# Two early row tiles instead of three in an attention kernel that hands its rows to a mixture of experts

## The chip, the cores and the metric

The kernel runs on one core of a Trainium2 chip. The metric is the device time of one execution in microseconds. Its engines are named TensorE (PE; its weight loads PEld), VectorE (DVE), ScalarE (ACT), GpSimd (POOL) and SyncE (SP). GpSimd and SyncE mostly issue transfers here.

## The reference

Attention over 8 batches, 12 heads, 448 tokens of 64 columns, with a root-mean-square norm of q and k, then a layer of 8 experts. Each token goes to the one expert that a hash of its id gives; the ids are inputs, so the table of rows is made on the chip.

```
q_n, k_n = rmsnorm(q, g_q), rmsnorm(k, g_k)
attn = softmax(scale * q_n @ k_n.T)
x = (attn @ v) as 3584 rows of 768 columns
expert_idx = token_ids * 2654435761 % 8
for e in range(8):
    mask = expert_idx == e
    h = relu(x[mask] @ w1[e])        # 768 -> 1024
    out[mask] = h @ w2[e]            # 1024 -> 768
```

## The kernel before

**Attention stage.** It walks 48 steps (8 batches of 6 pairs of heads). The order of all engines' work is written out by hand as a text of tokens (`steady`): `sc` scores, `exp`, `av` the output with the row sums, `rec` and `x` the normalisation into `x_sb`. TensorE, VectorE and ScalarE execute in that order; a transfer stands in the queue of the engine that issues it, and an engine that waits holds up what is queued behind it. After a batch's sixth step `put_x` calls `store_x`, which writes the batch's 448 rows to `x_scratch` in device memory. Partition p of the lower half holds the left columns of its seven tokens first, so the rows are stored as four pieces: three tokens from the lower 64 partitions, three from the upper, and the middle token's two halves. `put_x` ends with `hooks(s + 1)`, which issues loads and, near the end, gathers.

**Rows of an expert.** Every expert has 4 row tiles (KT) of 128 places (CAP = 512), of which 480 (FIT) are computed. The last tile is gathered as 96 rows. A table `gidx` holds the token of each place. Tokens of batches 0 to 6 come first, and those of batch 7 start at place EARLY or behind the earlier ones, whichever is later. So the tiles below EARLY hold no row of batch 7 and can be gathered before the last batch is stored. In a gather, N_EARLY as the row bound tells the framework that only rows of batches 0 to 6 are read; with N it waits for the last store. `gather` is an indirect DMA of GpSimd; `put_xT` turns a gathered tile with six transposes on TensorE and one copy (VectorE, or ScalarE where `nc.scalar.copy` is given).

**The seam.** The table of experts 0 and 1 is ready near the end of attention. Expert 0's early tiles are gathered by `hooks` into `xg_e` and turned by `early_xT`, ahead of the last step's `av`, in the PSUM banks of the scores. Then come the last `av`, `put_x` with the last store, and the gathers of expert 1's early tiles into `xg_ring`; then, in the expert stage, `fetch` of the tiles that need batch 7.

**Expert stage.** For each expert `gemm1` makes h, 8 blocks of 128 hidden units over the row columns; `gemm2` makes one row tile of the output in two parts (512 and 256 columns), evacuates it (ScalarE for even, VectorE for odd tiles) and scatters it. Expert 0 is special: `gemm1` covers the columns below EARLY, and `gemm1_late` the rest, right before its third row tile. `plan` says behind which block (`"g"`) or row tile (`"k"`) the work on the full table of experts 2 to 7 is emitted (p3 to p11, low, high, table_mm). `before` and `between` say what TensorE does before a row tile of `gemm2`, or between its two parts: mostly `turn`, the transposes of a row tile that is needed later (`t0` with the copy on ScalarE). All row tiles turned in this stage go through one PSUM bank (`ps_x`). Weights are loaded by GpSimd (`load_w1`, `load_w2`, `w_next`).

Of the kernel before, what the change touches and what calls it, by code (L numbers as in the profile page):

```python
# [13 lines left out]
AF = mybir.ActivationFunctionType  # L14
# [6 lines left out]
def kernel(  # L21
# [35 lines left out]
    EARLY = CAP - P  # L57
# [204 lines left out]
    with tc.manual_schedule(), \  # L262
# [369 lines left out]
        def early_xT(kt):  # L632
            bank = ps_sc.tile([P, 2, 512], FP32, name="sc_ps")[:, 0]
            put_xT(xg_e[:, kt], xT_e, kt, bank.bitcast(FP16)[:, 0:DIN],
                   nc.scalar.copy if kt == KT - 2 else None)
# [62 lines left out]
        def store_x(b):  # L698
# [3 lines left out]
            def rows(tok0, cnt, col, width):  # L702
                return bass.AP(tensor=x_dram.tensor, offset=(r0 + tok0) * DIN + col,
                               ap=[[SL * DIN, 64], [1, cnt * width]])
            nc.sync.dma_start(out=rows(0, 3, 0, DIN),
                              in_=x_sb[0:64, 0:6, :].rearrange("p a c -> p (a c)"))
            eng = nc.gpsimd if b == B - 1 else nc.sync
            eng.dma_start(out=rows(4, 3, 0, DIN),
                              in_=x_sb[64:P, 0:6, :].rearrange("p a c -> p (a c)"))
            nc.sync.dma_start(out=rows(3, 1, 0, HW), in_=x_sb[0:64, 6, :])  # L710
            eng.dma_start(out=rows(3, 1, HW, HW), in_=x_sb[64:P, 6, :])
# [80 lines left out]
        def hooks(s):  # L792
# [11 lines left out]
            if NS - 4 <= s < NS - 5 + KT:  # L804
                c = s - NS + 4
                gather(xg_e[:, c], gidx[:, c:c + 1], N_EARLY)
# [97 lines left out]
        for kt in range(KT - 1):  # L904
            early_xT(kt)
        for part in range(3):
            av_part(NS - 1, part)
        row_sums(NS - 1)
        put_x(NS - 1)
        for c in range(KT, 2 * KT - 1):  # L910
            gather(xg_ring[:, c], gidx[:, c:c + 1], N_EARLY)


    with tc.manual_schedule(), \
# [14 lines left out]
        def gemm1_late(w1v, xT, h_sb, c0, c1):  # L929
            n = c1 - c0  # L930
            for f0 in range(0, FO, 4):
                h_ps = ps_h.tile([P, 512], FP32, name="h_ps")
                for i in range(4):
                    for co in range(CO):
# [3 lines left out]
                nc.scalar.activation(h_sb[:, f0:f0 + 4, c0:c1],  # L938
                                     h_ps[:, 0:4 * n].rearrange("p (i t) -> p i t", i=4), AF.Relu)
# [43 lines left out]
        xgs = {c: xg_ring[:, c] for c in range(KT, 2 * KT - 1)}  # L983
        xTs = {0: xT_e}

        def fetch(e, kts):
            for kt in kts:
# [3 lines left out]
                                N_EARLY if kt < KT - 1 else N)  # L991
# [165 lines left out]
        def each(f, *parts):  # L1157
# [3 lines left out]
            (0, "g", 0): [tok16], (0, "g", 1): [p3], (0, "g", 2): [p4, p5], (0, "g", 3): [p6],  # L1161
            (0, "g", 4): [p7, p8], (0, "g", 5): [p9, p10, p11],
            (0, "g", 6): each(low, 0, 1), (0, "g", 7): each(low, 2, 3), (0, "k", 0): [high],
# [9 lines left out]
        before[0, 0], before[0, 1] = [t0(1, 0)], [t0(0, KT - 1)]  # L1173
        between[0, 1] = t0(1, 1)
# [4 lines left out]
        fetch(0, [KT - 1])  # L1179
        fetch(1, [KT - 1])  # L1180
# [78 lines left out]
```

## Time and profile before

| what | us |
|---|---|
| median of 3 runs (345.2 to 347.8) | 345.54 |
| profiled execution, its own time | 343.94 |
| its span, first to last instruction | 342.4 |
| TensorE busy in the span | 327.5 |
| VectorE, ScalarE, GpSimd busy | 201.8, 188.6, 147.7 |
| expert 0's first matmul starts | 163.26 |
| expert 1's first matmul starts | 186.50 |

The profile is one execution taken by the hardware profiler. Its span is 1.5 us shorter than the execution's own time. A busy TensorE says that matmuls were under way, not that they ran at their peak. Where an engine waits, the profile names what released it, or "issue" if it shows no wait. A landing time runs from the start of the issuing instruction to the completion of the transfer.

### The profile page before, as it was taken

How to read it: one execution, taken by the hardware profiler on the slowest of the kernel's cores; microseconds unless marked ns; L12 is line 12 of the kernel's file. 1: busy time of each engine (PE TensorE's matmuls, PEld its weight loads, DVE VectorE, ACT ScalarE, POOL GpSimd, SP SyncE). 2: the span in 40 equal slices, each digit the busy share in tenths (PEclk: the TensorE clock that was granted, in tenths of full speed). 3: DMA queues.
4: the chain of work that ended last, by engine and by line, in shares of the span. 5: the costliest groups of instructions: out<-in, count | busy, mean ns of one | idle time of the engine just before them, and what ended most of it. 6: DMA issues, size and time to landing. Idle time of an engine off the chain costs nothing. (4 is left out here: it accounts for less than half of the span.)

```text
span 342.4 us, 9198 instructions
## 1 busy us (share of the span) xinstructions
PE 327.5 (96%) x3893; PEld 228.6 (67%) x3893; DVE 201.8 (59%) x433; ACT 188.6 (55%) x286; POOL 147.7 (43%) x203
## 2 busy tenths in 40 slices
PE   4999999999999999999999999999999999999992
PEld 2577777776777777666677767677676776767761
DVE  3799999998989899976693243232332323323210
ACT  3599999999999999989442212212122120220210
POOL 8799935225330100003555854538555474202122
PEclk9999999999999999999999999999999999999997
DMA  8999999999999999032579899999999999403012
GB/s 138 217 200 202 202 236 200 239 202 227 201 244 211 254 210 233 13 82 71 127 147 247 169 204 249 261 278 244 252 272 262 259 243 278 174 0 133 22 79 88
DMA packets 42498, 64.80 MB, mean 189 GB/s; under 512 B 9687, under 2 KB 30623, under 8 KB 42200
## 3 DMA queue, kind: packets, MB, share of 16 engines
q0 software_dynamic: 38688, 58.09, 84.1%
q1 hardware_dynamic: 3456, 5.90, 5.6%
q8 instruction: 31, 0.51, 0.6%
q10 hardware_dynamic: 312, 0.21, 0.2%
q14 instruction: 11, 0.09, 0.1%
HBM read 89.29 MB, written 17.30 MB: 311 GB/s over the span
## 5 line engine op out<-in xcount | busy, mean ns | idle before, releaser
L642 ACT ACTIVATE expT<-sc_ps 128x896 bf16<-128x896 f32 x144 | 125.5, 973 | 1.6 <-PE sc_ps L626 1.3
L962 PEld LDWEIGHTS <-h_sb 128*128 128x128 f16 (+1 forms) x512 | 51.2, 104 | 30.0
L962 PE MATMUL o_ps<-w_sb,h_sb 128*128 128x512 f16 (+3 forms) x384 | 66.2, 326 | 0.0
L975 POOL DMA_INDIRECT out_dram<-o_sb,gidx x32 | 33.9, 1058 | 65.2 <-ACT o_sb L972 31.3
L949 ACT ACTIVATE h_sb<-h_ps 128x480 f16<-128x480 f32 (+1 forms) x36 | 19.9, 552 | 68.1 <-PE h_ps L945 68.1
L229 POOL DMA_INDIRECT kr<-x_scratch,gidx x32 | 33.5, 1047 | 52.1 <-DVE gidx L557 37.8
L945 PEld LDWEIGHTS <-w_sb 128*128 128x128 f16 x288 | 38.9, 136 | 16.2
L945 PE MATMUL h_ps<-xT,w_sb 128*128 128x480 f16 x240 | 49.4, 366 | 0.0
L972 ACT COPY o_sb<-o_ps 128x768 f32<-128x768 f32 x16 | 12.8, 798 | 61.4 <-PE o_ps L962 61.4
L951 DVE TENSOR_SCALAR h_sb<-h_ps 128x480 f16<-128x480 f32 x28 | 18.4, 658 | 47.2 <-PE h_ps L945 47.2
L626 PE MATMUL sc_ps<-qT,kT 64*128 64x448 f16 x288 | 44.5, 356 | 1.4 <-ACT expT L642 0.7
L660 PEld LDWEIGHTS <-expT 128*128 128x128 bf16 x864 | 37.8, 97 | 10.1 <-DVE x_sb L691 4.4
L660 PE MATMUL av_ps<-v,expT 128*128 128x65 bf16 x864 | 43.3, 193 | 0.1
L972 DVE COPY o_sb<-o_ps 128x768 f32<-128x768 f32 (+1 forms) x15 | 14.3, 956 | 31.5 <-PE o_ps L962 27.2
L691 DVE TENSOR_TENSOR x_sb<-av_ps,srec 128x448 f16<-128x448 f32 x48 | 29.9, 622 | 1.4
L303 POOL DMA_DIRECT2D vr<-in_v_dram x36 | 23.8, 671 | 15.6 <-DMA kr<-in_k_dram 6.8
L645 ACT ACTIVATE expT<-sc_ps 128x448 bf16<-128x448 f32 x48 | 29.4, 613 | 0.0
L384 PEld LDWEIGHTS <-ident 128*128 128x128 f16 x576 | 23.0, 99 | 8.5 <-issue 4.8
L241 DVE COPY xT<-xT_ps 128x768 f16<-128x768 f16 x25 | 13.8, 552 | 22.6 <-PE xT_ps L240 22.4
L665 PE MATMUL av_ps<-v,expT 128*128 128x130 bf16 x144 | 25.0, 220 | 0.0
L962 PE MATMUL o_ps<-kr,h_sb 128*128 128x512 f16 (+3 forms) x128 | 22.1, 326 | 0.0
L626 PEld LDWEIGHTS <-kT 64*128 64x128 f16 x288 | 12.6, 93 | 11.4 <-issue 2.5
(211 smaller groups left out, 453.0 us busy)
## 6 DMA issues: line engine op xcount, KB each, us to landing
w_sb<-in_moe_w_dram POOLq DMA_DIRECT2D x18, 512.0 KB, 10.9
w_sb<-in_moe_w_dram POOLq DMA_DIRECT2D x8, 768.0 KB, 13.7
kr<-in_k_dram POOLq DMA_DIRECT2D x7, 672.0 KB, 14.3
qr<-in_q_dram POOLq DMA_DIRECT2D x7, 672.0 KB, 12.5
x_scratch<-x_sb SPq DMA_DIRECT2D x15, 288.0 KB, 6.1
w_sb<-in_moe_w_dram POOLq DMA_DIRECT2D x2, 1536.0 KB, 26.5
qr<-in_moe_w_dram POOLq DMA_DIRECT2D x6, 512.0 KB, 15.6
vr<-in_v_dram POOLq DMA_DIRECT2D x14, 192.0 KB, 11.7
```

The source lines that it names most:

```text
L229: nc.gpsimd.indirect_dma_start(out=xg[0:idx.shape[0], :], out_offset=None, in_=x_dram[0:rows, :], in_offset=bass.IndirectOffsetOnAxis(ap=i ...
L303: eng.dma_start(out=dst[64 * half:64 * half + 64, :, s0:s0 + cnt, :].rearrange("p n s d -> p n (s d)"), in_=runs(t, h0 + HP * hh, 1, n, to ...
L626: nc.tensor.matmul(sc[:, hh, :S], lhsT=kT[64 * hh:64 * hh + 64, P * j:P * j + P], rhs=qT[64 * hh:64 * hh + 64, :], start=True, stop=True)
L642: nc.scalar.activation(expT[:, 2 * j:2 * j + 2, :], sc[:, :, :S], AF.Exp, bias=0.0, scale=1.0)
L645: nc.scalar.activation(expT[:, 6, :], sc[:, 0, :S], AF.Exp, bias=0.0, scale=1.0)
L660: nc.tensor.matmul(av[:, 2 * t + hh, :], lhsT=expT[:, tl(hh, j), P * t:P * t + P], rhs=v8[:, i, vs(hh, j), 0:D + 1], start=(hh == 0 and t ...
L665: nc.tensor.matmul(av[:, 2 * t:2 * t + 2, :], lhsT=expT[:, 6, P * t:P * t + P], rhs=v8[:, i, 0::7, 0:D + 1], start=False, stop=False)
L691: nc.vector.tensor_tensor(out=xs[b][:, :, hp * D:hp * D + D], in0=av[:, :, :D], in1=srec[:, :, None].to_broadcast([P, SL, D]), op=ALU.mult)
L945: nc.tensor.matmul(h_ps[:, :c1 - c0], lhsT=w1v[:, co, fo, :], rhs=xT[:, co, c0:c1], start=(co == 0), stop=(co == CO - 1))
L962: nc.tensor.matmul(o_ps[d0 > 0][0:w, d0:d1], lhsT=h_sb[:, fo, col * P:col * P + w], rhs=w2_sb[:, fo, d0:d1], start=(fo == 0), stop=(fo == ...
L972: (nc.vector.tensor_copy if col % 2 else nc.scalar.copy)(o_sb[0:w], o_ps[0][0:w])
L975: scat = nc.gpsimd.indirect_dma_start(out=out[:, :], out_offset=bass.IndirectOffsetOnAxis(ap=idx[0:w], axis=0), in_=o_sb[0:w], in_offset=N ...
```

## The change

EARLY falls from 384 to 256 places, so two tiles of each expert are free of batch 7 instead of three. Of expert 0 two tiles are gathered and turned ahead of the last step's output, and its third and fourth tile are gathered behind the last store; they are turned between the parts of `gemm2`'s first tile and before its second. `gemm1` of expert 0 covers 256 columns and `gemm1_late` 224, in four evacuations of two blocks. Expert 1's two early gathers are issued right behind the early transposes, ahead of the last step's output, and its other two tiles behind the last store. `store_x` writes three runs instead of four pieces, all from SyncE; in the last batch two of the four were GpSimd's. Pieces of the table's work move to other blocks of expert 0. For experts 2 to 7 the third tile's gather has the row bound N.

```diff
--- before.py
+++ after.py
@@ -54,7 +54,8 @@
     NOV = 32
     NHI = E * KT + NOV
     BIG = 1 << 20
-    EARLY = CAP - P
+    NE = KT // 2
+    EARLY = NE * P
     PL = P - P // B
     EH = E // 2
     KM = EH * NTC
@@ -632,7 +633,7 @@
         def early_xT(kt):
             bank = ps_sc.tile([P, 2, 512], FP32, name="sc_ps")[:, 0]
             put_xT(xg_e[:, kt], xT_e, kt, bank.bitcast(FP16)[:, 0:DIN],
-                   nc.scalar.copy if kt == KT - 2 else None)
+                   nc.scalar.copy if kt == NE - 1 else None)
 
         def expo(s, j):
             if j == 0:
@@ -702,13 +703,11 @@
             def rows(tok0, cnt, col, width):
                 return bass.AP(tensor=x_dram.tensor, offset=(r0 + tok0) * DIN + col,
                                ap=[[SL * DIN, 64], [1, cnt * width]])
-            nc.sync.dma_start(out=rows(0, 3, 0, DIN),
-                              in_=x_sb[0:64, 0:6, :].rearrange("p a c -> p (a c)"))
-            eng = nc.gpsimd if b == B - 1 else nc.sync
-            eng.dma_start(out=rows(4, 3, 0, DIN),
+            nc.sync.dma_start(out=rows(0, SL, 0, HW),
+                              in_=x_sb[0:64].rearrange("p a c -> p (a c)"))
+            nc.sync.dma_start(out=rows(4, 6, 0, HW),
                               in_=x_sb[64:P, 0:6, :].rearrange("p a c -> p (a c)"))
-            nc.sync.dma_start(out=rows(3, 1, 0, HW), in_=x_sb[0:64, 6, :])
-            eng.dma_start(out=rows(3, 1, HW, HW), in_=x_sb[64:P, 6, :])
+            nc.sync.dma_start(out=rows(3, 1, HW, HW), in_=x_sb[64:P, 6, :])
 
 
         def load(b, kinds="kqv"):
@@ -801,7 +800,7 @@
                 load(4, "kv")
             if hp == 3 and 1 <= b and b + 4 < B:
                 load(b + 4, "qkv")
-            if NS - 4 <= s < NS - 5 + KT:
+            if NS - 4 <= s < NS - 4 + NE:
                 c = s - NS + 4
                 gather(xg_e[:, c], gidx[:, c:c + 1], N_EARLY)
             if s == 24:
@@ -901,14 +900,14 @@
         """
         for b in range(2, B):
             emit(steady, b)
-        for kt in range(KT - 1):
+        for kt in range(NE):
             early_xT(kt)
+        for c in range(KT, KT + NE):
+            gather(xg_ring[:, c], gidx[:, c:c + 1], N_EARLY)
         for part in range(3):
             av_part(NS - 1, part)
         row_sums(NS - 1)
         put_x(NS - 1)
-        for c in range(KT, 2 * KT - 1):
-            gather(xg_ring[:, c], gidx[:, c:c + 1], N_EARLY)
 
 
     with tc.manual_schedule(), \
@@ -928,15 +927,16 @@
 
         def gemm1_late(w1v, xT, h_sb, c0, c1):
             n = c1 - c0
-            for f0 in range(0, FO, 4):
+            m = 512 // n
+            for f0 in range(0, FO, m):
                 h_ps = ps_h.tile([P, 512], FP32, name="h_ps")
-                for i in range(4):
+                for i in range(m):
                     for co in range(CO):
                         nc.tensor.matmul(h_ps[:, n * i:n * i + n], lhsT=w1v[:, co, f0 + i, :],
                                          rhs=xT[:, co, c0:c1],
                                          start=(co == 0), stop=(co == CO - 1))
-                nc.scalar.activation(h_sb[:, f0:f0 + 4, c0:c1],
-                                     h_ps[:, 0:4 * n].rearrange("p (i t) -> p i t", i=4), AF.Relu)
+                nc.scalar.activation(h_sb[:, f0:f0 + m, c0:c1],
+                                     h_ps[:, 0:m * n].rearrange("p (i t) -> p i t", i=m), AF.Relu)
 
         def gemm1(w1v, xT, h_sb, c0, c1, both=True, after=()):
             for fo in range(FO):
@@ -980,7 +980,7 @@
                 tc.declare_no_dep(scat.ins, group="scatters", reason="disjoint rows")
                 tc.add_to_no_dep_group("scatters", scat.ins)
 
-        xgs = {c: xg_ring[:, c] for c in range(KT, 2 * KT - 1)}
+        xgs = {c: xg_ring[:, c] for c in range(KT, KT + NE)}
         xTs = {0: xT_e}
 
         def fetch(e, kts):
@@ -988,7 +988,7 @@
                 c = e * KT + kt
                 xgs[c] = gather(xg_ring[:, c % (2 * KT)],
                                 gidx[0:P if kt < KT - 1 else LAST, c:c + 1],
-                                N_EARLY if kt < KT - 1 else N)
+                                N_EARLY if kt < NE else N)
 
         def turn(e, kt, copy=None):
             if e not in xTs:
@@ -1158,9 +1158,9 @@
             return [lambda p=p: f(p) for p in parts]
 
         plan = {
-            (0, "g", 0): [tok16], (0, "g", 1): [p3], (0, "g", 2): [p4, p5], (0, "g", 3): [p6],
-            (0, "g", 4): [p7, p8], (0, "g", 5): [p9, p10, p11],
-            (0, "g", 6): each(low, 0, 1), (0, "g", 7): each(low, 2, 3), (0, "k", 0): [high],
+            (0, "g", 0): [tok16], (0, "g", 1): [p3], (0, "g", 2): [p4, p5], (0, "g", 5): [p6],
+            (0, "g", 6): [p7, p8], (0, "g", 7): [p9, p10, p11] + each(low, 0, 1),
+            (0, "k", 0): each(low, 2, 3) + [high],
             (0, "k", 1): [high_tok], (0, "k", 2): [table_mm, lambda: fetch(2, range(KT))],
             (1, "k", 0): [overflow_table],
         }
@@ -1170,14 +1170,14 @@
         for e in range(1, E - 1):
             for kt in range(KT):
                 before[e, kt] = [t(e + 1, kt)]
-        before[0, 0], before[0, 1] = [t0(1, 0)], [t0(0, KT - 1)]
-        between[0, 1] = t0(1, 1)
+        before[0, 0], between[0, 0] = [t0(1, 0)], t0(0, 2)
+        before[0, 1], between[0, 1] = [t0(0, 3)], t0(1, 1)
         before[0, 2] = [lambda: gemm1_late(w1_view(0, w_tiles[0][0]), xTs.pop(0), hs[0], EARLY, FIT)]
         between[0, 2] = t0(1, 2)
         before[0, 3] = [t(1, 3)]
         hs = {}
-        fetch(0, [KT - 1])
-        fetch(1, [KT - 1])
+        fetch(0, range(NE, KT))
+        fetch(1, range(NE, KT))
         load_w2(2, w_tiles[2][1])
         queue += w_pieces(3)
         for e in range(E):
```

GpSimd's queue at the end of attention, with the semaphores each row waits for (kr_68 is `xg_e`, kr_69 is `xg_ring`; DMAHW are SyncE's stores, DMASW GpSimd's own transfers). Before:

```order
L229 DMA kr_68<-x_scratch,gidx 128x768 [waits DMASW3_49]
L708 DMA x_scratch<-x_sb 64x2304 [waits DMASW4_49,DVE_49]
L711 DMA x_scratch<-x_sb 64x384 [waits DMASW5_49]
L229 DMA kr_69<-x_scratch,gidx 128x768 [waits DMASW6_49]
L229 DMA kr_69<-x_scratch,gidx 128x768 [waits DMASW7_49]
L229 DMA kr_69<-x_scratch,gidx 128x768 [waits DMASW0_49]
L229 DMA kr_69<-x_scratch,gidx 96x768 [waits DMAHW3_49,DMASW5_49,DMAHW4_49,DMASW4_49,DMASW1_49]
L229 DMA kr_69<-x_scratch,gidx 96x768 [waits DMASW2_49]
```

The same place of the changed kernel:

```order
L230 DMA kr_68<-x_scratch,gidx 128x768 [waits DMASW2_49]
L230 DMA kr_69<-x_scratch,gidx 128x768 [waits DMASW3_49]
L230 DMA kr_69<-x_scratch,gidx 128x768 [waits DMASW4_49]
L230 DMA kr_69<-x_scratch,gidx 128x768 [waits DMAHW5_49,DMAHW6_49,DMAHW4_49,DMASW5_49]
L230 DMA kr_69<-x_scratch,gidx 96x768 [waits DMASW6_49]
L230 DMA kr_69<-x_scratch,gidx 128x768 [waits DMASW7_49]
L230 DMA kr_69<-x_scratch,gidx 96x768 [waits DMASW0_49]
```

The row that waits for the last batch's stores was the fourth behind them and is now the first behind two early gathers of expert 1; four tiles stand from it on instead of two.

TensorE between the two parts of `gemm2` of expert 0's first row tile, before:

```order
L962 LDWEIGHTS h_sb [waits Activation_49]
L962 MATMUL o_ps<-w_sb,h_sb 128x512
L962 LDWEIGHTS h_sb
L962 MATMUL o_ps<-w_sb,h_sb 128x256
L962 LDWEIGHTS h_sb
```

The same place of the changed kernel:

```order
L962 LDWEIGHTS h_sb [waits Activation_49]
L962 MATMUL o_ps<-w_sb,h_sb 128x512
L241 LDWEIGHTS kr_69 [waits DMASW5_49]
L241 MATMUL xT_ps<-ident_75,kr_69 128x128 [waits Activation_49]
L241 LDWEIGHTS kr_69
```

The transposes of expert 0's third tile stand between the parts now, and wait for the gather that waits for the stores.

## Rows read from the trace of the kernel before

**Rows 1.** Busy us (xcount) of PE, PEld, DVE, ACT, POOL; clock, DMA share, GB/s.
```profile
163.26:186.50 23.24, 23.15 (x231) 15.97 (x226) 16.33 (x39) 9.70 (x17) 13.38 (x12) 1.00 0.74 169
186.50:336.80 150.30, 149.04 (x930) 101.96 (x928) 45.50 (x70) 27.71 (x43) 68.54 (x76) 1.00 0.79 199
```

**Rows 2.** Timeline of TensorE at the seam: start us, length us, line, what, count.
```profile
161.35 1.00 PE L240 MATMUL sc_ps<-ident,kr 128*128 128x128 f16 x12 [0.41 <-DMA kr<-x_scratch,gidx]
...
162.19 0.53 PE L660 MATMUL av_ps<-v,expT 128*128 128x65 bf16 x12
...
163.26 2.12 PE L945 MATMUL h_ps<-xT_e,w_sb 128*128 128x384 f16 x12
...
165.22 0.22 PE L1051 MATMUL h_ps<-sel,onehot 128*112 128x2 bf16 x2
...
167.49 4.06 PE L945 MATMUL h_ps<-xT_e,w_sb 128*128 128x384 f16 x24
...
171.65 0.51 PE L240 MATMUL xT_ps<-ident,kr 128*128 128x128 f16 x6
...
171.99 2.77 PE L962 MATMUL o_ps<-w_sb,h_sb 128*128 128x512 f16 x16
...
174.59 0.50 PE L240 MATMUL xT_ps<-ident,kr 128*128 128x128 f16 x6
...
177.87 2.20 PE L935 MATMUL h_ps<-xT_e,w_sb 128*128 128x96 f16 x48
...
179.91 1.89 PE L962 MATMUL o_ps<-w_sb,h_sb 128*128 128x512 f16 x8
...
186.50 9.88 PE L945 MATMUL h_ps<-xT,w_sb 128*128 128x480 f16 x48
```

**Rows 3.** Timeline of TensorE's weight loads, third early tile.
```profile
161.84 0.34 PEld L240 LDWEIGHTS <-kr 128*128 128x128 f16 x6 [0.15 <-DMA kr<-x_scratch,gidx]
```

**Rows 4.** Timeline of ScalarE: last exp, copy of the third early tile.
```profile
161.03 0.62 ACT L645 ACTIVATE expT<-sc_ps 128x448 bf16<-128x448 f32 x1
...
162.39 0.80 ACT L241 COPY xT_e<-sc_ps 128x768 f16<-128x768 f16 x1 [0.74 <-PE sc_ps L240]
```

**Rows 5.** Timeline of VectorE: index table, last x, end of the routing's work.
```profile
154.29 0.33 DVE L557 CAST gidx<-val 64x8 int32<-64x8 f32 x2
...
163.61 0.62 DVE L691 TENSOR_TENSOR x_sb<-av_ps,srec 128x448 f16<-128x448 f32 x1
...
183.76 0.21 DVE L1138 TENSOR_SCALAR emp<-h_ps 128x56 f32<-128x56 f32 x1 [3.04 <-PE h_ps L1136]
```

**Rows 6.** Timeline of SyncE's queue: its two pieces of the last store.
```profile
164.26 0.45 SPq L705 DMA_DIRECT2D x_scratch<-x_sb  x1
...
164.75 0.60 SPq L710 DMA_DIRECT2D x_scratch<-x_sb  x1
```

**Rows 7.** Timeline of GpSimd: the first two gathers.
```profile
154.92 1.13 POOL L229 DMA_INDIRECT kr<-x_scratch,gidx  x1 [37.75 <-DVE gidx L557]
...
156.35 1.02 POOL L229 DMA_INDIRECT kr<-x_scratch,gidx  x1 [0.30 <-issue]
```

**Rows 8.** The gathers' line L229, 154 to 173 us (eight gathers); POOLq is GpSimd's sequencer.
```profile
L229 POOLq EVENT_SEMAPHORE  x2: 43/996/1948, 167.4 to 169.4; - x2
...
DMA to landing us min/median/max: 2.9/3.8/5.0
```

**Rows 9.** The same view, first gather alone, then the second alone.
```profile
DMA to landing us min/median/max: 3.2/3.2/3.2
...
DMA to landing us min/median/max: 5.0/5.0/5.0
```

**Rows 10.** Tile x_sb, its stores: SyncE's last two; the last four; all 32.
```profile
DMA to landing us min/median/max: 2.9/3.0/3.1
...
DMA to landing us min/median/max: 2.9/3.3/3.8
...
DMA to landing us min/median/max: 2.9/6.2/8.6
```

## Prediction

> **What bounds the kernel now.** I read the busy time by stretches first, since a share of the whole says nothing of one seam [rows 1]. From the first matmul of expert 0 to that of expert 1 TensorE works 23.15 of 23.24 us, and from there to its end 149.04 of 150.30 us, all at granted clock 1.00. TensorE is the bound on both sides of the edit, so only TensorE's own work or waits there change the end; what the other engines save is worth nothing.
>
> Then TensorE's order of time at the seam [rows 2]. The reader is to see two gaps and the pace of each kind of work. The gaps: transposes of early tile 1 begin only at 161.35 us, released by their gather, and the first transposes of expert 1 at 171.65 us, although the 24 matmuls from 167.49 us are out by 167.49 + 24 x 0.1633 = 171.41 us; 0.24 us are lost there. The pace: 12 matmuls of 384 columns take 163.26 to 165.22, 0.1633 us each; 48 of 96 columns 177.87 to 179.91, 0.0425 each; six transposes 171.65 to 171.99, 0.34; a pass of gemm2 171.99 to 174.59, 2.60, two thirds of it (1.73) the 512 columns and 0.87 the 256.
>
> Last I read the chain that the change leans on, attention output to gathered rows: VectorE ends the last x at 163.61 + 0.62 = 164.23 [rows 5], SyncE stores at 164.26 and 164.75 [rows 6], GpSimd's gathers follow [rows 7, 8], and the landings [rows 8 to 10].
>
> **Part 1, one early tile less ahead of the last step.** Six transposes leave the place before the last attention output. Tile 1 still waits to 161.35 [rows 2], as its gather keeps its place and its 5.0 us [rows 7, 9]. Before, tile 2's weight loads began at 161.84 [rows 3] and the output's matmuls 0.35 later, at 162.19 [rows 2]; now they follow tile 1 by the same 0.35, at 161.70. Gain 0.49 us, and gemm1 starts at 163.26 - 0.49 = 162.77. ScalarE bounds the gain: its last exp ends at 161.65, the copy of the last early tile takes 0.80 and ended 0.07 ahead of gemm1 [rows 4], so gemm1 can't start before 162.52, a gain of 0.74 at most; if tile 1's gather lands 0.5 later, since two gathers stand behind it instead of one, it is 0. I take 0.49, as the landing of the same gather is in the trace. The six transposes come back between the halves of gemm2's first pass: +0.34.
>
> **Part 2, other columns.** Expert 0's columns split 256 + 224 instead of 384 + 96. At the pace of the 384-column row, 48 x 0.1089 = 5.23 and 48 x 0.0953 = 4.57, together 9.80; before 48 x 0.1633 + 2.04 = 9.88. That is -0.08; by the 96-column pace for the late ones (0.0425/96 x 224 = 0.0992 each) it would be +0.11. The four evacuations of the late part instead of two are ScalarE's, each under 12 matmuls (1.14 us) against some 0.6 us: nothing while that cover stands.
>
> **Part 3, expert 1's gathers ahead.** They leave GpSimd right behind the two early ones [rows 7], near 157.8 us, and with even 5.0 us [rows 9] land five microseconds ahead of need, so the 0.24 us go. VectorE's table work keeps its order, and it stood idle 3.04 us for TensorE at its end [rows 5]: that cover hides the regrouped plan.
>
> Without any new wait the sum is -0.49 + 0.34 - 0.08 - 0.24 = -0.47 us.
>
> **Part 4, the new wait.** Expert 0's tiles 2 and 3 are now both gathered behind the store of the last batch, and needed sooner. TensorE comes to tile 2 at 162.77 + 5.23 + 0.31 (the routing's small matmuls: 171.65 - 163.26 - 48 x 0.1633 - 0.24) + 0.34 + 1.73 = 170.38 us. The rows come: x ends at 163.74; SyncE issues at 163.77, 164.26 and 164.90 (0.49 and 0.60 + 0.04 apart [rows 6]). A store on this queue, idle at this place, took 2.9 to 3.1, with GpSimd's two 2.9 to 3.8 [rows 10]; the last piece is the small one, whose row is the 2.9: it lands at 167.8. GpSimd stands waiting there, where before its sequencer's wait of 1.95 us to 169.4 lay under the gathers ahead [rows 8]. From the index table's end at 154.62 [rows 5] to its gather at 154.92 [rows 7] a release took 0.30, so the first late gather starts at 168.1. The first gather of a burst on an idle queue landed after 3.2 [rows 9]: 171.3, and TensorE waits 0.9. The second starts 1.43 later [rows 7], at 169.5; the two nearest prices are 5.0 (second of that burst [rows 9]) and 2.9 (the shortest of eight), and I take the median of the eight, 3.8 [rows 8]: 173.3. TensorE is there at 171.3 + 0.34 + 0.87 = 172.5 and waits 0.8. Together 1.7 us.
>
> Bounds of this term: with store 2.9, no release time and 2.9 for each gather, the second lands at 167.8 + 1.43 + 2.9 = 172.13, against 171.59 of an unstalled TensorE: 0.54. With 3.8 for the last store and 5.0 for the second gather it lands at 168.7 + 0.3 + 1.43 + 5.0 = 175.4: 3.8. The start of gemm1 shifts both sides alike and doesn't change it. Behind the waiting gather on GpSimd stand three gathers, expert 2's w2 load and the scatters; expert 1's late tiles are needed some 8 us after they land, w2 two experts later, and the scatters are waited for by nobody here, so nobody else waits.
>
> All batches' stores now have three pieces instead of four. None of them is waited for in the attention stage, where SyncE has nothing else to issue; if that cover were gone, 7 x 0.6 us of issue saved would be the most it could give. I take nothing.
>
> **Sum:** -0.47 + 1.7 = +1.2 us. The profiled execution's own time is 343.94 us, 1.5 around its span of 342.4 and 1.6 below the median of 345.54; I put the difference on the median: 346.8 us. About 1% (3.5 us) is what a measurement of this kernel can tell from no change.
>
> **Rivals.** (a) The late rows land in time. TensorE would have to find tile 2 by 170.38 and tile 3 by 171.59; the shortest prices (170.7 and 172.13) miss by 0.3 and 0.5. For it: the store's packets are longer and nothing else is under way. Against it: not one of eight gathers was below 2.9. It gives -0.47, 345.1 us. The Trainium skill, "DMA: Bandwidth & Descriptors", section "Anatomy of one DMA — SWDGE (gpsimd) path", puts a DMA at some 2.0 us plus its bytes at 436 GB/s. Estimated by that rule the 48 KB store would take 2.1 and a gather of 192 KB 2.45, the rows would land at 169.8 and 171.2, and this rival would hold; the trace disagrees, with 2.9 for that store and 3.2 for the quiet gather. Chance 0.20.
>
> (b) Slower: the two dependent DMAs at their long ends. The mechanism is the same chain, store, release, second gather, at 3.8 and 5.0, and with the gain of part 1 gone as well: +0.02 + 3.8 = +3.8, 349.3 us. It decides for slower from tile 3 landing 3.9 us after the unstalled TensorE comes for it (with part 1's gain kept). For it: the second gather of the one quiet burst did take 5.0, and stores in the loaded attention stage took 6.2 in the median and up to 8.6 [rows 10]. Against it: no load is under way here. Chance 0.10.
>
> (c) The change doesn't shorten the front: tile 1's landing slips to where tile 2's was, and all else goes as forecast. +0.49 more, 347.3 us. Chance 0.10.
>
> **How the numbers follow.** The forecast (wait of 0.5 to 3 us, 345.5 to 348) has 0.57; something unseen that gains over 1% has 0.03, as no row shows 3.5 us to be had. 8 times in 10: from rival (a) and a little of run scatter, 344.9, to near the upper bound, 348.9. Within 1% lie the forecast, (a) and (c): 0.87; slower 0.10, faster 0.03.
>
> **What the new profile would show.** gemm1's 256-column matmuls from about 162.8; no idle ahead of expert 1's first transposes; SyncE's three stores from 163.8; a GpSimd gather released by a store near 168; TensorE idle some 0.9 and 0.8 us before the transposes of expert 0's tiles 2 and 3; expert 1's first matmul near 187.7 instead of 186.50, and the rest of the program equal. I am wrong if no idle stands before those transposes (a), if it exceeds 3.9 us (b), or if the later experts' stretch changes its 150.30 us.

## The result, and the profile after

| | median us | ratio to before, 95% interval |
|---|---|---|
| kernel before | 345.72 | |
| changed kernel | 349.26 | 1.0101 [1.0073, 1.0128] |
| changed kernel, timed a second time (before 344.52) | 347.07 | 1.0075 [1.0053, 1.0097] |

The change makes the kernel slower: 3.5 us in the first comparison, 2.6 us in the second. The forecast was +1.2, and 348.9 us as the upper end; 349.26 lies above it. What both intervals allow is 1.0073 to 1.0097, +2.5 to +3.3 us.

Where it is lost shows first in the busy time by stretches of the changed kernel (columns as in [rows 1]): expert 0's first matmul to expert 1's first, then from there on to the end of the later experts' work.

```profile
167.69:193.06 25.37, 23.64 (x236) 18.83 (x232) 15.86 (x39) 10.84 (x20) 11.35 (x9) 1.00 0.65 146
193.06:343.20 150.14, 149.05 (x930) 101.93 (x928) 45.52 (x70) 27.71 (x43) 68.44 (x76) 1.00 0.79 200
```

The second stretch is as long as before (150.30 in [rows 1]). In the first TensorE, idle for 0.09 of 23.24 us before, is idle for 1.73 of 25.37. Its timeline there answers to [rows 2]:

```profile
167.69 1.49 PE L945 MATMUL h_ps<-xT_e,w_sb 128*128 128x256 f16 x12
...
173.60 1.89 PE L962 MATMUL o_ps<-w_sb,h_sb 128*128 128x512 f16 x8
177.21 0.51 PE L241 MATMUL xT_ps<-ident,kr 128*128 128x128 f16 x6 [1.72 <-DMA kr<-x_scratch,gidx]
177.56 1.04 PE L962 MATMUL o_ps<-w_sb,h_sb 128*128 128x256 f16 x8
178.60 0.49 PE L241 MATMUL xT_ps<-ident,kr 128*128 128x128 f16 x6
178.94 1.89 PE L962 MATMUL o_ps<-w_sb,h_sb 128*128 128x512 f16 x8
...
181.87 4.76 PE L935 MATMUL h_ps<-xT_e,w_sb 128*128 128x224 f16 x48
...
193.06 1.18 PE L945 MATMUL h_ps<-xT,w_sb 128*128 128x480 f16 x5
```

The wait stands where the forecast put it, ahead of the transposes of expert 0's third tile: the eight 512-column matmuls are out by 173.60 + 1.73 = 175.33, the transposes begin at 177.21, 1.88 later (the row's 1.72 counts from the modelled end of the last matmul). Ahead of the fourth tile's transposes nothing waits for a gather. The 0.17 us lost there (177.56 + 0.87 = 178.43 to 178.60) go to the one PSUM bank that both tiles are turned through: ScalarE's copy of the third tile empties it at 177.75 + 0.80 = 178.55 (ScalarE's timeline):

```profile
177.75 0.80 ACT L242 COPY xT_e<-xT_ps 128x768 f16<-128x768 f16 x1 [3.16 <-PE xT_ps L241]
```

The cause of the wait for the third tile is in the queues. SyncE's timeline (answers to [rows 6]):

```profile
168.69 0.45 SPq L706 DMA_DIRECT2D x_scratch<-x_sb  x1
169.18 0.60 SPq L708 DMA_DIRECT2D x_scratch<-x_sb  x1
169.82 1.01 SPq L710 DMA_DIRECT2D x_scratch<-x_sb  x1
```

GpSimd's timeline, the first early gather and the first two late ones (answers to [rows 7]):

```profile
156.37 1.13 POOL L230 DMA_INDIRECT kr<-x_scratch,gidx  x1 [37.76 <-DVE gidx L558]
...
174.10 1.00 POOL L230 DMA_INDIRECT kr<-x_scratch,gidx  x1 [12.65 <-DMA x_scratch<-x_sb]
175.40 0.98 POOL L230 DMA_INDIRECT kr<-x_scratch,gidx  x1 [0.30 <-issue]
```

From the first store's issue to the gather that the stores release are 5.41 us. The forecast had 4.33 (163.77 to 168.1).

One thing in this execution is not part of the change. In the last attention steps VectorE stands still for 2.46 us, ScalarE for 1.66 and TensorE for 2.00, and TensorE's granted clock is 0.50 behind it (163.20 to 166.62), 1.2 of 2.4 GHz. TensorE's timeline:

```profile
163.19 0.84 PE L661 MATMUL av_ps<-v,expT 128*128 128x65 bf16 x12 [2.00 <-DVE x_sb L692]
```

Call the time from the start of the first gather to expert 0's first matmul the front, and that from there to expert 1's first matmul the seam. No other profile of a changed kernel has the standstill; all have a front of 7.74 to 7.78 us, against 163.26 - 154.92 = 8.34 before and 11.32 here. The parts of the change are therefore read from the second execution of the unchanged file, below.

### The profile page after: what moved, and what is told of

Same layout as the page of the kernel before. It is cut to its first block, busy times and chain, and to the rows that moved or that the text cites. A ratio compares the mean times of both kernels' runs of the same rounds, so it can differ in the third digit from the quotient of the medians.

```text
span 348.8 us, 9194 instructions
## 1 busy us (share of the span) xinstructions
PE 329.6 (95%) x3893; PEld 232.8 (67%) x3893; DVE 201.9 (58%) x432; ACT 190.2 (55%) x289; POOL 147.5 (42%) x201
## 5 line engine op out<-in xcount | busy, mean ns | idle before, releaser
L949 ACT ACTIVATE h_sb<-h_ps 128x480 f16<-128x480 f32 (+1 forms) x36 | 19.0, 528 | 66.3 <-PE h_ps L945 60.3
L945 PE MATMUL h_ps<-xT,qr 128*128 128x480 f16 x96 | 19.8, 366 | 0.0
```

What stands on the lines that cost most here:

```text
L945: nc.tensor.matmul(h_ps[:, :c1 - c0], lhsT=w1v[:, co, fo, :], rhs=xT[:, co, c0:c1], start=(co == 0), stop=(co == CO - 1))
```

## Experiments

Two families: names with b_ are the kernel before with one part of the change, names with a_ are the changed kernel with one thing undone or doubled. Medians of before differ by up to 1.2 us from one set of runs to another, so ratios are compared.

### Parts of the change alone: b_store3 and b_burst4

b_store3 gives the kernel before the three-run store and nothing else; b_burst4 only sends expert 1's first gather out ahead of the last output.

```diff
# b_store3, against before: store_x as in the change
-            eng = nc.gpsimd if b == B - 1 else nc.sync
...
+            nc.sync.dma_start(out=rows(3, 1, HW, HW), in_=x_sb[64:P, 6, :])
# b_burst4, against before
             early_xT(kt)
+        gather(xg_ring[:, KT], gidx[:, KT:KT + 1], N_EARLY)
...
-        for c in range(KT, 2 * KT - 1):
+        for c in range(KT + 1, 2 * KT - 1):
```

> The kernel before with the three runs of the store from SyncE alone, nothing else. GpSimd has no store between its gathers any more, so six gathers stand in a row: three of expert 0 and three of expert 1. Burst theory: the front, 8.3 us before from the first gather to gemm1, grows by as much as in the changed kernel or more (to 11 us or above), and the time is 2 to 4 us above before. Rival (the stores, or nothing): the front stays within 0.7 us of 8.3, and the time within 0.7 us of before; if the shorter stores cost the attention stage something, its earlier batches are later too.

> The kernel before with expert 1's first gather issued ahead of the last step's output: four gathers in a row, the store with GpSimd as before, three early tiles. Burst theory: the front grows from 8.3 by 1 to 3 us, the time is 1 to 3 us above before although the 0.24 us wait ahead of expert 1's first transposes is gone. Rival: the front stays, and the time is 0 to 0.5 us below before.

Measured: b_store3 0.9992 [0.997, 1.0013], b_burst4 0.9995 [0.9974, 1.0016], both with the front at 8.18 us and the seam at 22.97. Neither part by itself costs anything that can be measured, and a burst of six gathers ahead of the output doesn't lengthen the front, so the burst theory falls here. Both seams are 0.27 us shorter than before, near the 0.24 of part 3. The chain is as long in b_store3 as in the changed kernel: SyncE's first issue at 163.96, the released gather at 169.30, 5.34 us. Only nobody waits for it there, since the kernel before needs those rows later (timeline of GpSimd, b_store3):

```profile
169.30 1.09 POOL L229 DMA_INDIRECT kr<-x_scratch,gidx  x1 [6.83 <-DMA x_scratch<-x_sb]
```

The four pieces on two queues are no sooner where they are kept: in b_burst4 x ends at 164.51 and the released gather starts 5.68 us later (GpSimd's timeline, b_burst4); in the profiles of the changed kernel it is 5.44 and 5.65.

```profile
170.19 0.98 POOL L229 DMA_INDIRECT kr<-x_scratch,gidx  x1 [1.53 <-DMA x_scratch<-x_sb]
```

### Fewer early gathers: a_burst3

```diff
-        for c in range(KT, KT + NE):
-            gather(xg_ring[:, c], gidx[:, c:c + 1], N_EARLY)
+        gather(xg_ring[:, KT], gidx[:, KT:KT + 1], N_EARLY)
```

> The changed kernel with three gathers in a row ahead of the last step's output, as before, instead of four: expert 1's second tile is gathered behind the store. Burst theory (four gathers back to back hold up TensorE, VectorE and ScalarE in the last steps of attention): the time from the first gather's start to gemm1's first matmul, 8.3 us before and 11.3 in the changed kernel, falls back to 8.3 or less, and the time falls by 1 to 2 us below 349.3. Rival (that loss is not of the burst: it belongs to the run, to the code's place, or to the stores): it stays near 11 us where it was, or comes and goes with no regard to the count of gathers, and the time stays within 0.7 us of 349.3.

Measured: 1.0080 [1.0048, 1.0111], no better than the changed kernel. The profiled execution is the slowest of six (350.17 us, median 347.68), and in it the wait is not shorter but longer. Timeline of TensorE, a_burst3:

```profile
174.79 0.51 PE L241 MATMUL xT_ps<-ident,kr 128*128 128x128 f16 x6 [2.85 <-DMA kr<-x_scratch,gidx]
...
176.73 0.82 PE L241 MATMUL xT_ps<-ident,kr 128*128 128x128 f16 x6 [0.56 <-DMA kr<-x_scratch,gidx]
177.35 3.05 PE L961 MATMUL o_ps<-w_sb,h_sb 128*128 128x512 f16 x8
```

Busy time of a_burst3 by stretches, the granted clock third from the end:

```profile
171.80:174.80 3.00, 0.15 (x2) 0.02 (x2) 2.97 (x4) 0.00 (x0) 2.69 (x2) 1.00 0.22 66
174.80:177.00 2.20, 1.64 (x17) 1.29 (x18) 2.20 (x3) 1.59 (x2) 1.78 (x2) 0.84 0.21 57
177.00:180.00 3.00, 3.00 (x13) 1.33 (x11) 0.69 (x1) 0.81 (x2) 2.50 (x3) 0.55 0.45 124
180.00:182.00 2.00, 2.00 (x22) 1.77 (x21) 0.35 (x1) 0.80 (x1) 1.52 (x2) 1.00 1.05 158
```

So the burst theory falls: the front is 7.74 us again, and with one gather fewer ahead of it the last store landed 3.8 us after its issue, at 170.03, as it does in the changed kernel (3.7, below). What was longer in this execution is the way from that landing to the gather, 1.6 us instead of 0.8; why stays open. Timeline of GpSimd, a_burst3:

```profile
171.63 1.00 POOL L230 DMA_INDIRECT kr<-x_scratch,gidx  x1 [11.46 <-issue]
```

A second cost appears, which no term of the forecast holds: behind the wait the granted clock falls to half, 1.2 of 2.4 GHz, and the eight 512-column matmuls take 2.89 us instead of 1.73, the transposes 0.62 instead of 0.34: 1.44 us more. It is not in every execution: this one has a mean granted clock of 0.993 and one other 0.989 (349.08 us), the remaining four 0.996 to 0.997 and 346.4 to 347.9 us.

### The late rows needed later: a_turn_later

```diff
-        before[0, 0], between[0, 0] = [t0(1, 0)], t0(0, 2)
-        before[0, 1], between[0, 1] = [t0(0, 3)], t0(1, 1)
+        before[0, 0], between[0, 0] = [t0(1, 0)], t0(1, 1)
+        before[0, 1], between[0, 1] = [t0(0, 2)], t0(0, 3)
```

> The changed kernel with one thing moved: TensorE turns expert 0's tiles 2 and 3 one place later each (expert 1's second tile takes the place between the halves of the first pass). Chain theory (the rows that wait for the store are late by 1.9 us, and that is the seam's loss): TensorE comes 1.2 us later to tile 2, so the wait falls from 1.7 to about 0.5 us or less; expert 0's stretch, first matmul to expert 1's first matmul, falls from 25.4 to near 24 us, and the time is 1.0 to 1.9 us below the changed kernel's 349.3, near 347.8. Rival (the loss of the changed kernel lies ahead of expert 0, between the gathers' issue and gemm1): the time stays within 0.7 us of 349.3, and the trace shows again some 3 us more than before from the first gather to gemm1.

Measured: 1.0017 [0.9999, 1.0036]. Two lines of order, with every store and gather left as it is, take back most of the loss, as the chain theory expected. A wait of 0.82 is left, and the seam is 188.93 - 164.45 = 24.48 us (TensorE's timeline):

```profile
174.28 0.51 PE L241 MATMUL xT_ps<-ident,kr 128*128 128x128 f16 x6 [0.82 <-DMA kr<-x_scratch,gidx]
```

### The changed kernel again, and with TensorE kept busy: a_again, a_fill

```diff
# a_again: the changed kernel, nothing edited
# a_fill: ahead of the third tile's transposes
+            for _ in range(10):
+                nc.tensor.matmul(ps[:], lhsT=ident16[:], rhs=hs[0][:, 0:2, 0:EARLY],
+                                 start=True, stop=True)
```

> The changed kernel itself, for a second trace. In its first trace the engines stood still for some 3 us ahead of expert 0 (from the first gather to gemm1 11.3 us), in the two variants with the same front they did not (7.7 us). Chain theory: the front is 7.7 us again, 0.6 below before, and expert 0's stretch is 26 to 28.5 us against 23.24 before: TensorE waits 2 to 3 us for the first gather behind the store, and its granted clock is at half for some microseconds after the wait. Rival (the front loses 3 us in most runs): the front is above 10 us again, and expert 0's stretch near 25.4.

> The changed kernel with ten matmuls of 512 columns, 2.16 us, that nobody reads, in front of the transposes that wait for the first late tile. They keep TensorE at work through most of the wait. Theory A (the wait costs twice: its own time and the clock that is at half behind it, 1.2 to 1.5 us): the clock stays at 1.00 through expert 0's stretch, and the time is 0.5 to 1.5 us below the changed kernel of the same call. Theory B (only the wait itself costs): the time is the same, or up to 0.5 us above where the wait is shorter than 2.16 us.

Measured: a_again 1.0075 [1.0053, 1.0097], a_fill 1.0058 [1.0035, 1.008]. TensorE's timeline in a_again, where the front has no standstill:

```profile
170.08 1.89 PE L962 MATMUL o_ps<-w_sb,h_sb 128*128 128x512 f16 x8
173.95 0.51 PE L241 MATMUL xT_ps<-ident,kr 128*128 128x128 f16 x6 [1.98 <-DMA kr<-x_scratch,gidx]
```

The same place in a_fill:

```profile
171.69 2.32 PE L1176 MATMUL h_ps<-h_sb,ident 128*128 128x512 f16 x10
173.85 0.50 PE L241 MATMUL xT_ps<-ident,kr 128*128 128x128 f16 x6
```

Both seams are 25.6 us (25.63 and 25.64): matmuls that nobody reads fill the wait and move nothing. The front is 7.74 us again, as expected for a_again, but the fallen clock that was expected with it isn't there: the clock is 1.00 all through this seam, so here the wait alone is the seam's loss. With TensorE kept busy the loss is 346.75 - 344.52 = 2.2 us, 0.3 less than without, which the intervals can't tell from nothing.

The three stores are the transfer that the wait is made of. DMA share and GB/s are the last two numbers of these stretches of a_again; the first store was issued at 165.18:

```profile
165.00:166.00 1.00, 1.00 (x15) 0.92 (x13) 0.28 (x2) 0.85 (x3) 0.00 (x0) 1.00 0.00 0
166.00:167.00 1.00, 1.00 (x12) 0.90 (x10) 0.90 (x6) 0.46 (x2) 0.00 (x0) 1.00 0.81 172
167.00:168.00 1.00, 1.00 (x11) 0.90 (x10) 0.86 (x6) 0.59 (x2) 0.00 (x0) 1.00 0.93 172
168.00:169.00 1.00, 1.00 (x13) 0.90 (x12) 0.79 (x7) 0.56 (x2) 0.00 (x0) 1.00 0.96 311
169.00:170.00 1.00, 1.00 (x14) 0.92 (x12) 0.93 (x3) 0.43 (x2) 0.00 (x0) 1.00 0.17 49
```

172 + 172 + 311 + 49 is 704 thousand bytes in some 3.2 us with the 16 DMA engines busy: nearly all of it the last batch's x (336 + 288 + 48 KB, 688 thousand bytes). The small third store, 48 KB, stands behind 624 KB. It was issued at 166.31 and landed 3.7 later, at 170.02; the two ahead of it landed 3.4 and 3.9 after their issue, the second at 169.53. The gather they release starts at 170.80. The stretch cut where the bytes start and stop to move:

```profile
166.20:169.45 3.25, 3.25 (x34) 2.92 (x32) 2.77 (x18) 1.69 (x5) 0.00 (x0) 1.00 0.89 217
```

So of the 5.62 us from the first issue to the released gather 1.02 pass before bytes move, 3.25 move them at 217 GB/s, 0.57 go by to the last landing (170.02) and 0.78 from there to the gather.

### VectorE or the issuing engine as the cause: a_table_late, a_act_store

The first moves VectorE's routing work behind the wait, in case it delays GpSimd's release; the second lets ScalarE issue the small third store.

```diff
# a_table_late
-            (0, "g", 6): [p7, p8], (0, "g", 7): [p9, p10, p11] + each(low, 0, 1),
-            (0, "k", 0): each(low, 2, 3) + [high],
+            (0, "k", 0): [p6, p7, p8, p9, p10, p11] + each(low, 0, 1, 2, 3),
# a_act_store
-            nc.sync.dma_start(out=rows(3, 1, HW, HW), in_=x_sb[64:P, 6, :])
+            (nc.scalar if b == B - 1 else nc.sync).dma_start(out=rows(3, 1, HW, HW), in_=x_sb[64:P, 6, :])
```

> The changed kernel with VectorE's work on the full table (from the rank on) moved behind the first pass of gemm2, so that VectorE is idle while GpSimd waits for the store and gathers the late tiles. Theory A (VectorE's work delays GpSimd: the gather starts 0.8 to 1.5 us after the store's landing where 0.3 was expected, and gathers take 1.7 to 2.3 us on GpSimd where 1.0 is usual): start after 0.3 to 0.5, each gather 1.0, TensorE's wait 0.5 to 1.2 us shorter, and the time 0.5 to 2 us below the changed kernel. Theory B (the delay is GpSimd's own): starts and lengths stay, the time stays within 0.5 us or is up to 1 us longer, if the table comes too late for its matmuls.

> The changed kernel with the last batch's third and smallest run of the store issued by ScalarE beside SyncE's two. Theory A (the store's landing is late because three issues stand in one queue, the third 1.13 us behind the first and 1.0 us long): it goes out at the first one's time, lands 0.7 to 1.1 us earlier, TensorE's wait is that much shorter, and the time 0.7 to 1.5 us below the changed kernel. Theory B (the two large runs land as late, 3.4 to 3.9 us after their issue): the last landing comes 0.2 to 0.4 us earlier at most, and the time stays within 0.5 us.

Measured: a_table_late 1.0117 [1.007, 1.0164], a_act_store 1.0063 [1.004, 1.0087]. With VectorE idle from 169 to 175 us the released gather comes 6.87 us after the first issue, not sooner, as the third store itself landed only 5.0 after its issue, at 170.8; TensorE waits 3.4 and its clock falls. From that landing to the gather it is 0.8 us as in a_again, so VectorE doesn't hold the release up. The late landing has a cause in the trace that isn't VectorE either: a 16 KB transfer of the instruction queue (DMA view, 168.73 to 168.86; 42.3% of 16 engines in 0.13 us make 0.88 us of one engine) starts among the third store's last packets. Then, from 168.86 to 169.59, none of that store's data moves, and the last four packets follow (DMA view, 169.59 to 169.96):

```profile
q8 instruction: 1, 0.02, 42.3%
...
DMA packets 5, 0.00 MB, mean 8 GB/s; under 512 B 1, under 2 KB 5, under 8 KB 5
```

That the four stood behind this transfer on one of the 16 engines is inferred from these times. VectorE's table work does go with longer gathers behind the released one. GpSimd's third and fourth late gathers in a_again, beside it:

```profile
173.39 1.73 POOL L230 DMA_INDIRECT kr<-x_scratch,gidx  x1 [0.30 <-DVE lo L1119]
175.43 1.64 POOL L230 DMA_INDIRECT kr<-x_scratch,gidx  x1 [0.30 <-issue]
```

The third in a_table_late, where VectorE does nothing:

```profile
174.17 1.03 POOL L230 DMA_INDIRECT kr<-x_scratch,gidx  x1 [0.30 <-issue]
```

In a_act_store the small store landed 1.2 us sooner, counted from the first issue, and the second large one, now the last, later, 4.4 after its issue; the gather still comes 5.72 after the first issue. So it isn't the place of the small store in SyncE's queue that sets the end. TensorE waits 1.68 and 0.58 here and its clock falls behind that; this profiled execution is the slowest of ten (349.19 us, median 347.07).

### The first store issued twice: a_store_twice

```diff
+            if b == B - 1:
+                nc.sync.dma_start(out=rows(0, SL, 0, HW, y_dram),
+                                  in_=x_sb[0:64].rearrange("p a c -> p (a c)"))
             nc.sync.dma_start(out=rows(0, SL, 0, HW),
```

> The changed kernel, with the last step's first store (336 KB) issued twice, first to a tensor that nobody reads. Theory of bytes (the small third store lands when the 624 KB ahead of it have been moved, at some 230 GB/s over the DMA engines): the last landing moves by 0.5 us of issue and about 1.5 us in all, the wait ahead of the transposes of expert 0's third tile grows from 2.0 to about 3.5 us, and TensorE's granted clock falls after it. Rival (each store lands at a delay of its own after its issue): 0.5 us more wait, no more.

Measured: 1.0215 [1.0169, 1.026]. TensorE's timeline, a_store_twice:

```profile
168.97 1.89 PE L966 MATMUL o_ps<-w_sb,h_sb 128*128 128x512 f16 x8
175.98 0.82 PE L242 MATMUL xT_ps<-ident,kr 128*128 128x128 f16 x6 [5.12 <-DMA kr<-x_scratch,gidx]
```

The wait grows by 3.1 us, from 1.98 to 5.12, where 1.5 was expected. The rival (0.5 more) falls. The bytes account for half: all but the last four packets have moved 5.86 us after the first issue (164.06 to 169.92), against 4.27 for all of them in a_again, 1.6 later and near what was expected. The other half is the stall seen in a_table_late: an instruction transfer starts at 169.77, nothing of the stores moves from 169.92 to 170.64, then come the last four packets (DMA view, 169.76 to 169.80 and 170.64 to 171.01):

```profile
q8 instruction: 1, 0.02, 137.3%
...
DMA packets 5, 0.00 MB, mean 8 GB/s; under 512 B 1, under 2 KB 5, under 8 KB 5
```

The last large store lands 6.6 after its issue, 0.8 behind these packets. The clock falls to 0.58 (mean of 174 to 175) while TensorE still stands idle and is 0.50 for some 5 us of work, which costs 2.25 more.

### The wait taken out, and the start: a_late_split, a_zero_early, a_split_zero

In nearly all profiles of a_ kernels the first attention output is written at 22.0 to 23.2 us, in those of before, b_store3 and b_burst4 at 21.0 to 21.6. VectorE's two copies of v take 0.9 to 2.0 us there instead of 0.62, beside zeroings on GpSimd. a_late_split takes out the seam's wait, a_zero_early is aimed at the start, a_split_zero does both.

```diff
# a_late_split: late columns in two pieces, each right behind its rows
+        before[0, 0], between[0, 0] = [t0(1, 0)], t0(1, 1)
+        between[0, 1] = t0(0, 2)
+        before[0, 2], between[0, 2] = [g1l(EARLY, 3 * P)], t0(0, 3)
+        before[0, 3], between[0, 3] = [t0(1, 2), g1l(3 * P, FIT)], t0(1, 3)
# a_zero_early
+        zero_kv(nc.gpsimd, v_bufs[1])
+        nc.gpsimd.memset(k_keep[:]...[:, :, 6 * PAIR:], 0.0)
         load(2, "kq")
-        zero_kv(nc.gpsimd, v_bufs[1])
-        nc.gpsimd.memset(k_keep[:]...[:, :, 6 * PAIR:], 0.0)
```

> The changed kernel, but expert 0's late columns come in two pieces, 256 to 384 ahead of its third tile's second product and 384 to 480 ahead of its fourth's, and each tile is transposed only there, so that the late rows are needed 3 us later than in the changed kernel. Theory of the wait (the late rows' chain of store, release and gather is 1.5 to 2.5 us longer than TensorE's other work covers): no wait on a gathered tile is left, the stretch from expert 0's first matmul to expert 1's falls from 25.6 to 23.3 to 23.7 us, and the run is 2.0 us under the changed kernel: about 0.3 us under the kernel before if the later start in the profiles is chance, about 0.7 us over it if that start is part of the change. Rival (the change costs at the seam for another reason, such as shared ports or more instructions): the stretch stays above 24.5 us.

> The changed kernel with GpSimd's three zeroings of the start ahead of the two loads that they followed, some 1.7 us earlier. Theory of the start (the first output is normalised 1 us later in every profile of a changed kernel because VectorE's two 1024-column copies of v run at half pace or less beside GpSimd's zeroings): the copies take about 0.63 us again, the first output is written 0.7 us earlier or more, and the time falls by 0.7 to 1.2 us against the changed kernel, to 1.004 of the kernel before. Rival (the later start is chance, or comes from something else): copies above 1.3 us or a first output still at 22.3 us, and a ratio of 1.0075 as before.

> Both edits, the split late columns and the earlier zeroings. If both theories hold: 0.3 us under the kernel before (ratio 0.999, between 0.997 and 1.000). If only that of the wait holds: the same as with the split alone.

Measured: a_late_split 0.9991 [0.997, 1.0012], a_zero_early 1.0063 [1.0039, 1.0087], a_split_zero 1.0004 [0.9983, 1.0025]. Expert 0's stretch of a_late_split:

```profile
164.18:187.96 23.78, 23.76 (x285) 18.95 (x280) 15.37 (x38) 11.76 (x21) 13.06 (x11) 1.00 0.63 130
```

TensorE is idle for 0.02 us, with stores, gathers, burst and front of the changed kernel all in place, and the time is that of the kernel before, as the theory of the wait expected. So the whole loss that can be measured is the wait and what follows from it. The start decides nothing that the medians show: a_late_split writes its first output at 22.48 and is as fast as before, so the later start belongs to single executions or is too small to be told in the medians. a_zero_early didn't test its theory of the start: GpSimd waits for transfers ahead of the zeroings, which came only 0.35 us earlier and met the copies again (1.56 us for two).

No version here beats both kernels; a_late_split equals the kernel before.

## Why the prediction was wrong, point by point

The sum of the forecast was -0.47 without a wait and +1.7 of waits. Against the a_again profile:

- **Part 1, the front.** Forecast -0.49 (bounds 0 and -0.74) and +0.34 for the moved transposes. Measured 8.34 to 7.74, -0.60. Right; the 0.1 more is tile 1's, whose gather landed after 4.8 instead of 5.0, so that its transposes waited for ScalarE's exp and not for the gather.
- **Parts 2 and 3.** From expert 0's first matmul to the first transposes behind its 256 columns it is 5.57 us (forecast 5.23 + 0.31 = 5.54), and the late 224 columns take 4.60 (4.57). No idle stands ahead of expert 1's first transposes. Without its waits the seam is 25.63 - 2.32 = 23.31 us against 23.24: +0.07, where +0.34 - 0.08 - 0.24 = +0.02 was forecast. Right.
- **Part 4, when TensorE is there.** Forecast 170.38 - 163.74 = 6.64 us after x ends, measured 171.81 - 165.15 = 6.66. Right.
- **Part 4, when the rows are there: the step that failed.** Forecast, from the end of x: stores issued within 1.16 us, the third lands 2.9 later, release 0.30, gather at 4.36, rows 3.2 later. Measured: issue within 1.16; landing after 3.7, at 4.87; gather at 5.65; rows 3.1 later, at 8.76. The store was sized 0.8 too short and the release 0.5 too short, and the first wait is 2.14 instead of 0.9. The 2.9 was a small store's row with 288 KB of SyncE's own ahead of it; here 624 KB stood ahead on one queue. The release of 0.30 was taken from VectorE to GpSimd; from the landing of a store it is some 0.8 in the profiles here, 1.6 in a_burst3. The whole chain was in the trace of before, if in four pieces on two queues: GpSimd's wait for the same 672 KB ended at 169.4 [rows 8], 5.2 us after x ended at 164.23 [rows 5]. I wrote that it lay under other gathers, and priced the parts anew instead of using it. With 5.2 and a gather's 3.2 the first wait is 1.8 and more. That this comes near is luck in part: 1.1 of the 5.2 passed before GpSimd issued its pieces, and the release behind the landing isn't in it; the changed kernel's 4.87 and 0.78 are other parts.
- **Part 4, the second wait.** Forecast 0.8, measured none for the rows: the second gather starts 1.30 after the first and lands in 2.8 rather than 3.8, at 174.94, before TensorE comes for it at 174.30 + 0.87 = 175.17. The 0.18 that TensorE loses there, to 175.35, are the PSUM bank's, as in the first profile, a term that the forecast didn't have. An error the other way, of 0.6; in a_act_store and a_turn_later the same gather took 3.7 and 3.8, as forecast, so the 2.8 is not settled by one profile. Both losses together are 2.32 against 1.7.
- **What no term held.** Behind such a wait the clock can halve: 1.4 us in a_burst3 (waits of 2.85 and 0.56), 2.25 in a_store_twice. a_act_store lost some 1.6 that way after 1.68 and 0.58, a_again nothing after 1.98. The waits forecast (0.5 to 3.8) reached into lengths where this happens, and the bounds should have held it.

So the profile of a_again gives -0.60 + 0.07 + 2.32 = +1.8 us, and some +3.2 where the clock falls, against a forecast of +1.2; what both timings allow is +2.5 to +3.3. The mean granted clock of every execution of a_again is 0.996 to 0.998, that of its profile 0.997, so it fell in none of them, and +1.8 lies at the low end of their +1.8 to +3.3. In the first comparison the executions have 0.988 to 0.998, the three at 0.988 and 0.989 took 349.4 to 350.9 us and the three at 0.997 and 0.998 took 348.0 to 349.1: there the clock did fall in some. It isn't all of the scatter, as the fastest and the slowest of the twelve (347.79 and 351.74) both have 0.993. What parts these two sets of executions of one file stays open. 349.3 us, the figure of rival (b), came out otherwise than by its steps: the last store did land near its 3.8, but part 1's gain was kept, and the second gather took 2.8, not 5.0. Rival (a) is excluded: it needed the third tile's rows 6.64 us after the end of x, and they came 8.76 after it. The prediction's estimate by the Trainium skill ("DMA: Bandwidth & Descriptors", "Anatomy of one DMA — SWDGE (gpsimd) path"), 2.1 us for the small store and 2.45 for a gather, is exceeded by both here, 3.7 and 3.1. The Trainium skill, "DMA: Bandwidth & Descriptors", section "Queues, rings and completion order", also states what bears on such a burst: a completion mark lands only after every earlier write of the same DMA engine, across queues. The trace agrees: the 48 KB land at 170.02, behind the 288 KB that landed at 169.53, and the burst's share of the 16 engines is above 0.8 for 3 us.

## What to carry to other kernels

Price a small store by the bytes that stand ahead of it on the DMA engines and not by its own size: here 48 KB took 3.7 us behind 624 KB, and 336 KB more in front moved the bytes by 1.6 us and, with an instruction transfer among the last packets, the reader by 3.1. When a dependent chain is already in the trace, take its end-to-end time (end of x to the end of GpSimd's wait for the stores: 5.2 us before the change) ahead of summing its parts, even where other work hides it today, and add the way from the landing to the reader. Before moving rows out of an early batch, move the place where the late rows are needed too: two lines of order took 1.0075 back to 1.0017, and a finer split to 0.9991.

## What the hardware showed that I had not expected

- TensorE's granted clock went from 1.00 to 0.50 (1.2 GHz) in or behind idle times of 2.00 us (the first profile of the changed kernel), 2.85 followed by 0.56 (a_burst3), 3.40 (a_table_late), 5.12 (a_store_twice), and 1.68 followed by 0.58 (a_act_store); behind 1.98 (a_again) it stayed at 1.00. So the length of the idle time alone doesn't tell it here.
- In a burst of stores on SyncE the third issue takes 1.01 us and a fourth 1.62 (a_store_twice), where the first takes 0.45 and the second 0.60.
- A gather's issue on GpSimd takes 1.0 us with VectorE idle and mostly 1.4 to 2.3 beside VectorE's table compares; a_again's second late gather ran beside the first of them in 0.98, where a_turn_later's took 1.91. The Trainium skill, "SBUF — State Buffer", section "Terms", has both engines share a pair of ports that one holds for a whole instruction. The longer rows agree, the 0.98 doesn't show it, and no run here separates that from another cause.
- From the last packet of the stores to the last landing it is 0.6 us in a_again, and from there to the gather 0.8. One 16 KB transfer of the instruction queue between a store's packets moved its landing by over 1 us in a_table_late and a_store_twice.
